# Batch 0's second two pairs turned by VectorE from block loads, with the last ordering, range checks, similarities and slopes at other places

## The chip, the cores and the metric

The kernel runs on one core of a Trainium2 chip. The core has five engines with queues of their own: TensorE (PE in the profile), VectorE (DVE), ScalarE (ACT), GpSimd (POOL) and SyncE (SP), which issues DMAs. [...] The metric is the device time in microseconds. Of the kernel before, three runs took 944.75, 945.04 and 946.84 us; the median is 945.04.

## The reference: what is computed

Routing attention and then a feed-forward block, all in fp32. There are 4 batches, 8 heads, 768 tokens and head dimension 64.

```python
q_n, k_n, c_n = (x / (norm(x) + 1e-6) for x in (q, k, centroids))
q_assign = argmax(q_n . c_n over 16 clusters);  k_assign likewise
scores = where(q_assign[:, None] == k_assign[None, :], q k^T / 8, -1e9)
x = softmax(scores) @ v              # heads side by side: (3072, 512)
h = x @ w_in                         # (3072, 2048)
out = (max(h, 0) + alpha * min(h, 0)) @ w_out    # (3072, 512)
```

A query attends to the keys of its own cluster alone. The weights and alpha are shared by all tokens; the weights come in as 64-bit floating-point numbers.

## The kernel before

**Pairs and steps.** Two heads of one batch make a pair, so there are 16 pairs n, four to a batch; one holds 768 queries and 768 keys of both heads. Pairs 0 to 9 are done whole (all keys against all queries, in two halves of 384 queries), pairs 10 to 15 are first sorted by cluster, so that only near blocks of keys and queries meet. The order of the work is written out by hand: a list of 78 steps (`steps`), three to a half of a pair (or to a sorted pair), 24 for each of the first two batches. A first loop runs steps -4 to 23 (batch 0), a second one steps 24 to 77. In each step pieces are put at slots: `tick()` counts the slots, `later(k, piece)` puts a piece k slots on, `prep_at[(step, slot)]` holds the preparation of pairs to come, `load_at[step]` holds loads, which are issued ahead of everything else in the step. The order in which pieces are emitted is the order on each engine's queue.

**A pair's way through the kernel.** `load` brings q and k of two heads into two tiles of a pool of four (`inp`); `load_v` brings v. The features must lie along the partitions for the scores. For pairs of batch 0 `prep_features` (lines 347 to 359) does this on TensorE, 24 products with an identity matrix in three groups, each copied from PSUM by ScalarE. For pairs of later batches the load writes blocks of 32 features and 32 tokens in such an order (line 127) that `prep_blocks` (364) needs one 32x32 block transpose on VectorE for each of q and k. Batch 0 numbers its tokens as partition times six plus j (the load at line 119 is two contiguous DMAs, one for q and one for k), later batches as j times 128 plus partition. `prep_sims` (381) multiplies features and centroids into a spare PSUM bank of `misc`, and `prep_argmax` finds clusters on VectorE (402 to 410). In batch 0 the members are turned (423), sent to other partitions by small DMAs that ScalarE issues (474), and made into a penalty by ScalarE (429), which TensorE adds to the scores (790). Then come `score` (781), exp on ScalarE (802), `weigh` (936) with sums of the denominators (in batch 0's first halves on TensorE, 929, read by VectorE at 942), and `normalise` (1039), which frees the one PSUM bank of the output products (`vps`) and fills a part of xT. `invert` (904) turns denominators into inverses; `inverse` calls `check_inverses` (340) at the first pair of a new batch, which takes the least and greatest of all inverses for a range check at the end.

**Weights.** They arrive in 32 chunks of 512 KB (`convert`, 247) in five raw tiles. A chunk is split by VectorE (253, 255), scaled by ScalarE (259, 261), joined by VectorE (265, 268) and GpSimd (271). In batch 0 these pieces stand between the attention's own on VectorE's queue; `fetch` issues a chunk's DMA on SP when a raw tile will be free. On SP the order at the start is: loads of pairs 0 and 1, chunks 0 to 2, v of pair 1, load(2), v of pair 2, chunks 3 and 4, load(3), chunks 5 and 6, v of pair 3, chunk 7 and so on.

**Feed-forward.** Once a half batch has its xT, its pieces (`hidden`, 1063, and `final`, 1081) are fed to TensorE between the attention's steps. The last batch's feed-forward works with sums of blocks and fewer products (`last_pieces`, 1241 and 1297). In its `hidden(x)`, two blocks of hidden units, f1 and f2, are made from products p1 to p7 and a deferred p4; `plus` (1176) adds a product from PSUM, `slopes` (1181) applies alpha.

**Sorting.** `ORDERS` gives the step at which a sorted pair's ordering begins: its load (line 127's form), two transposes (565), `order_sims` (573), counts and a scan (587), `order_begins` (599), `order_rows`. This puts 18 stage loads (659, on SP) and 24 scatters (673, on POOL) into a queue, `sorting`, from which the steps take as room allows; `order_load` (694) brings the rows back sorted, before the pair's first step.

Of the kernel before, what the change touches and what calls it, by code (L numbers as in the profile page):

```python
# [19 lines left out]
P = 128  # L20
# [3 lines left out]
def kernel(  # L24
# [11 lines left out]
    nc = tc.nc  # L36

    B, H, S, D = q.shape
    NC = centroids.shape[1]
    DM, DF = moe_w_in.shape  # L40
    NJ = S // P
    NCH = DM // P
# [52 lines left out]
    def later(slots, piece):  # L95
        due.setdefault(now[0] + slots, []).append(piece)
# [7 lines left out]
    pairs = [(b, hp) for b in range(B) for hp in range(NCH)]  # L104
# [3 lines left out]

    Q = 32

    def load(n):

        b, hp = pairs[n]
        for w, src in enumerate((q, k)):
            raw = inp.tile([P, 2, NJ, D], FP32, name="qk")
            if n < NCH:
                nc.sync.dma_start(
                    out=raw.rearrange("p h j d -> p h (j d)"),  # L120
                    in_=src[b, 2 * hp:2 * hp + 2].rearrange("h (p j) d -> p h (j d)",
                                                            j=NJ))
            for h in range(2):
                rows = src[b, 2 * hp + h]
                for x in range(D // Q if n >= NCH else 0):
                    r = h * D + x * Q
                    nc.sync.dma_start(
                        out=raw.rearrange("p h j d -> p (h j d)")[r:r + Q, :].rearrange(
                            "p (t i) -> p t i", i=Q),
                        in_=rows[:, x * Q:(x + 1) * Q].rearrange("(t p) i -> p t i", p=Q))  # L130
            raw_qk[n, w] = raw
# [30 lines left out]
    for g in range(P // Q):  # L162
        r = slice(g * Q, (g + 1) * Q)
        nc.gpsimd.tensor_copy(
            out=fold[r, :].rearrange("p (a i) -> p a i", i=Q),
            in_=ident[r, None, r].broadcast_to((Q, P // Q, Q)))
# [11 lines left out]
    for h in range(2):  # L178
        nc.vector.tensor_reduce(
            out=pick[:, h:h + 1],  # L180
            in_=fold.rearrange("p (a h c) -> p a h c", h=2, c=NC)[:, 0, h, :],
# [142 lines left out]
    lowest = const.tile([P, B], FP32, name="lowest")  # L324
    highest = const.tile([P, B], FP32, name="highest")
    WORDS = [float((127 + e) * 2 ** 23) for e in (-50, 40)]
    kept_of = [0]

    def inverse(n, half):

        if pairs[n][0] > kept_of[0]:
            check_inverses()
        return inverses[:, (2 * n + half) % (2 * NCH), :]

    def check_inverses():
        i = kept_of[0]
        kept_of[0] += 1
        words = inverses.bitcast(I32).rearrange("p n x -> p (n x)")
        for to, op in ((lowest, ALU.min), (highest, ALU.max)):
            nc.vector.tensor_reduce(out=to[:, i:i + 1], in_=words, axis=AX.X, op=op)  # L340
# [20 lines left out]
    def prep_blocks(n, w):  # L361
        if w == 0:
            qkTs[n] = qkp.tile([P, NB * P], FP32, name="qkT")
        nc.vector.transpose(out=qkTs[n][:, w * S:(w + 1) * S],
                            in_=raw_qk[n, w].rearrange("p h j d -> p (h j d)"))
# [11 lines left out]
    def prep_sims(n):  # L377
        hp = pairs[n][1]
        ps = misc()
        for g in range(NG):  # L380
            nc.tensor.matmul(out=ps[g * W:(g + 1) * W, 0:HS],  # L381
                             lhsT=cT[:, hp * W:(hp + 1) * W],
                             rhs=qkTs[n][:, g * HS:(g + 1) * HS],
                             start=True, stop=True)
        later(1, lambda: prep_argmax(n, ps))
# [753 lines left out]
    def last_pieces():  # L1139
        b = B - 1  # L1140
# [34 lines left out]
        def plus(to, of):  # L1175
            nc.vector.tensor_tensor(out=to, in0=to, in1=of, op=ALU.add)

        def slopes(f):
            halves, both = g[f]
            for t in halves if both is None else [both]:  # L1180
                nc.vector.scalar_tensor_tensor(out=t, in0=t, scalar=alpha[:, f:f + 1], in1=t,
                                               op0=ALU.mult, op1=ALU.max)
# [50 lines left out]
        def hidden(x):  # L1233
            f1, f2 = x, NQ + x
            bank = {}

            def product(to, m, rhs, start):
                if start:
                    bank[to] = new_bank(to)[:, 0:HS]
                for cc in range(KH):  # L1240
                    nc.tensor.matmul(out=bank[to], lhsT=w_in_form(m, x, cc),  # L1241
                                     rhs=rhs[:, cc, :], start=start and cc == 0,
                                     stop=cc == KH - 1, skip_group_check=not start)
                return bank[to]

            def x_of(half, kh):
                return xTs[b, half][:, kh * KH:(kh + 1) * KH]

            def g_of(f, half):
                return g[f][0][half]  # L1250

            def p1():
                if not g:
                    places()
                copy(g_of(f1, 0), product("a", "11", x_of(0, 0), True))

            def p5():
                copy(g_of(f2, 1), product("e", "S1", x_sums[0], True))

            def p2():  # L1260
                plus(g_of(f1, 0), product("z", "12", x_of(0, 1), True))
                if late:
                    late.popleft()()

            def p6():
                copy(g_of(f1, 1), product("a", "S2", x_sums[1], False))

            def p3():
                plus(g_of(f1, 1), product("e", "S4", x_of(1, 1), False))
                slopes(f1)  # L1270

            def p7():
                plus(g_of(f2, 1), product("a", "S3", x_of(1, 0), False))
                late.append(p4)
                if x % 2 == 0 and x:
                    g_sums(x - 2)
                    w_out_sums(x - 2)
                    if x // 2 + 1 < NQ // 2:
                        w_in_sums(x // 2 + 1)
                elif x > 1:  # L1280
                    g_sums(x - 2)
                    w_out_sums(x - 2)

            def p4():
                copy(g_of(f2, 0), product("a", "22", x_sums[2], False))
                slopes(f2)
            return [p1, p5, p2, p6, p3, p7]
# [72 lines left out]
    SLOTS, FIRST = 5, 2  # L1360
# [2 lines left out]
    FREE = SLOTS * SB - 3  # L1363


    ORDERS = [26, 29, 35, 38, 41, 50]
    prep_at, load_at = {}, {}
    for (n, half), u in start_of.items():
        def at(step, slot, piece):
            prep_at.setdefault((step, slot), []).append(piece)  # L1370
        if half is None:
            t = ORDERS[n - NO]
            load_at.setdefault(t, []).append(lambda n=n: load(n))
            for i in range(2):
                at(t + 1, FIRST + i, lambda n=n, i=i: order_features(n, i))
            at(t + 2, 2, lambda n=n: order_sims(n))
            load_at.setdefault(u - (3 if n == NO + 1 else 4), []).append(
                lambda n=n: order_load(n))
            at(u - 4, 0, lambda n=n: prep_clusters(n))
            for i in range(2):  # L1380
                at(u - 1, i, lambda n=n, i=i: order_blocks(n, i))
                at(u - 1, FIRST + i, lambda n=n, i=i: order_queries(n, i))
            continue
        if half == 0:
            if n < NCH:
                if n > 1:
                    load_at.setdefault(max(u - 7, 0), []).append(lambda n=n: load(n))
                if n > 0:
                    load_at.setdefault(max(u - 6, 0), []).append(lambda n=n: load_v(n))
            else:  # L1390
                load_at.setdefault(u - 9, []).append(lambda n=n: load(n))
                load_at.setdefault(u - 7, []).append(lambda n=n: load_v(n))
            if n < NCH:
                for g in range(len(groups)):
                    at(u - 4, FIRST + g, lambda n=n, g=g: prep_features(n, g))
            else:
                for w in range(2):
                    at(u - 7, FIRST + w, lambda n=n, w=w: prep_blocks(n, w))
            at(u - (3 if n < NCH else 5 if u - 6 < TOGETHER else 6), FIRST,
               lambda n=n: prep_sims(n))  # L1400
            if n >= NCH:
                at(u - 4, FIRST if u - 4 < TOGETHER else 0, lambda n=n: prep_clusters(n))
        if n < NCH:

            if half == 1 or n == 0:
                at(u - (3 if half else 1), FIRST,
                   lambda n=n, half=half: prep_queries(n, half, 0))
            continue
        for h in range(2):
            at(u - 1, FIRST + h, lambda n=n, half=half, h=h: prep_queries(n, half, h))  # L1410
# [385 lines left out]
```

## Time and profile before

| | |
|---|---|
| profiled execution | 944.23 us, span of its instructions 942.5 us |
| median of three runs | 945.04 us |
| TensorE, VectorE, ScalarE, GpSimd busy | 98%, 70%, 28%, 37% of the span |
| granted TensorE clock | 0.999 |
| line 354, the 192 records of turning by TensorE | 8.6 and 4.2 us busy by tile, 277 and 272 ns each |
| line 364, the 12 transposes of later batches | 11.4 us, 947 ns each |
| line 1063 and 1081, feed-forward products | 257.7 and 254.4 us busy |
| line 340, a check's two reductions | 0.21 to 0.25 us each, first at 224.5, last at 789.8 us |
| queue of SyncE and its engines' share | 201840 packets, 60.35 MB, 29.2% |

A matmul in fp32 appears as two records, so the 24 products of a pair are 48. Records overlap on TensorE: the mean of one is longer than the distance between two. "Idle before" counts from the end of the engine's previous work, and names what ended the wait. An instruction of SP in the timeline is the issue of a DMA; its window is not the transfer. Times in the timeline count from the span's start.

### The profile page before, as it was taken

The numbers are of one execution on the slowest core, as the hardware profiler recorded it, in microseconds if no ns is written. First come the engines' busy times: TensorE is split into PE (matmuls) and PEld (weight loads), VectorE is DVE, ScalarE is ACT, GpSimd is POOL, SyncE is SP. The second block draws the span as 40 slices with busy tenths as digits, with TensorE's granted clock in tenths as the row PEclk, the third lists the DMA queues.
The fourth block names the chain that finished last, engine by engine and source line by source line (L and its number), as shares of the span: only waits on it lengthen the run. The fifth ranks groups of instructions, "written<-read, shape, count | busy, mean of one in ns | idle before, by whom it ended". The sixth has DMA issues, their size and how long they took to land.

```text
span 942.5 us, 11891 instructions
## 1 busy us (share of the span) xinstructions
PE 924.1 (98%) x3995; PEld 496.5 (53%) x3995; DVE 663.5 (70%) x1247; ACT 265.9 (28%) x658; POOL 351.2 (37%) x529
## 2 busy tenths in 40 slices
PE   8999999999999999999999999999999999999997
PEld 5534444445455454454544545545455555556886
DVE  5797788799679589698995955456888535698100
ACT  5764444323123032331322322223133121221000
POOL 2333222200016576467534686364256670000000
PEclk9999999999999999999999999999999999999999
DMA  8333658039001645165920134333441112000000
GB/s 297 125 127 96 146 130 149 18 59 198 1 6 53 159 87 133 47 120 131 155 52 12 43 80 101 63 67 62 93 75 34 32 37 53 1 0 1 23 23 26
DMA packets 209668, 73.38 MB, mean 78 GB/s; under 512 B 194288, under 2 KB 198080, under 8 KB 209600
## 3 DMA queue, kind: packets, MB, share of 16 engines
q1 hardware_dynamic: 201840, 60.35, 29.2%
q0 software_dynamic: 6912, 11.81, 4.1%
q8 instruction: 33, 0.54, 0.2%
q10 hardware_dynamic: 848, 0.39, 0.2%
q14 instruction: 35, 0.29, 0.1%
HBM read 49.89 MB, written 22.28 MB: 77 GB/s over the span
## 4 chain that ended last, share of the span: by engine, by line
PE 87%; DVE 6%; SPq 2%; DMA 2%; issue 1%; POOL 1%; ACT 1%; ACTq 0%; DVEq 0%; POOLq 0%
PE fps L1081 26%; PE fps L1063 25%; PE vps L936 7%; PE sps L781 7%; PE sps L1297 4%; PE sps L1241 4%; PE fps L781 2%; PE vps L1297 2%; PE vps L1241 2%; PE fps L1297 1%; PE fps L1241 1%; PE sps L790 1%; PE vps L969 1%; PE mps L969 1%; PE mps L381 1%
## 5 line engine op out<-in xcount | busy, mean ns | idle before, releaser
L1063 PE MATMUL fps<-xT,w_in_sb 128*128 128x384 f32 x768 | 257.7, 490 | 0.0
L1081 PE MATMUL fps<-w_out_sb,gT 128*128 128x512 f32 x576 | 254.4, 595 | 1.1 <-DVE gT L1055 1.1
L1063 PEld LDWEIGHTS fps<-xT,w_in_sb 128*128 128x128 f32 x768 | 142.8, 190 | 102.6 <-issue 3.8
L1081 PEld LDWEIGHTS fps<-w_out_sb,gT 128*128 128x128 f32 x576 | 107.5, 190 | 133.4 <-issue 123.0
L673 POOL DMA_INDIRECT scratch<-stage,off x144 | 155.4, 1079 | 49.7 <-issue 25.1
L650 POOL COPY paced<-pace 1x1 f32<-1x1 f32 x196 | 55.5, 283 | 202.3 <-ACT pace L649 201.5
L1069 ACT COPY gT<-fps 128x384 f32<-128x384 f32 x96 | 46.0, 479 | 215.6 <-PE fps L1063 215.6
L1055 DVE SCALAR_TENSOR_TENSOR gT<-gT,alpha 128x384 f32<-128x384 f32 x96 | 61.3, 648 | 50.4 <-ACT gT L1069 50.3
L781 PE MATMUL sps<-qkT 64*128 64x384 f32 (+1 forms) x480 | 88.6, 487 | 0.0
L1008 POOL DMA_INDIRECT back<-rows,found x72 | 74.9, 1040 | 18.2 <-issue 16.1
L802 ACT ACTIVATE E<-sps 128x768 f32<-128x768 f32 (+1 forms) x78 | 57.9, 790 | 59.4 <-PE sps L790 38.8
L781 PEld LDWEIGHTS sps<-qkT 64*128 64x128 f32 x480 | 42.7, 186 | 40.5 <-issue 15.0
L822 DVE SCALAR_TENSOR_TENSOR more<-aq,key,more 128x384 f32<-128x384 bf16 (+2 forms) x120 | 63.0, 584 | 1.2 <-ACT more L799 1.1
L936 PE MATMUL vps<-E,vt 128*64 128x384 f32 x316 | 58.6, 495 | 1.4 <-DVE xT L1039 1.4
L904 DVE RECIPROCAL inverses<-mps 64x12 f32<-64x12 f32 (+1 forms) x44 | 10.9, 248 | 58.5 <-PE mps L891 58.1
L822 DVE SCALAR_TENSOR_TENSOR E<-aq,key,E 128x384 f32<-128x384 bf16 (+2 forms) x96 | 50.2, 577 | 1.9 <-ACT E L799 1.8
L271 POOL TENSOR_TENSOR w_in_sb<-w_in_sb,power 128x512 f32<-128x512 f32 x16 | 25.1, 1573 | 67.8 <-DVE w_in_sb L268 67.8
L832 DVE TENSOR_TENSOR acc<-acc,E 128x768 f32<-128x768 f32 x37 | 35.3, 953 | 14.7 <-ACT E L802 13.6
L271 POOL TENSOR_TENSOR w_out_sb<-w_out_sb,power 128x512 f32<-128x512 f32 x16 | 22.9, 1434 | 57.3 <-DVE w_out_sb L268 57.3
L802 ACT ACTIVATE more<-sps 128x768 f32<-128x768 f32 (+1 forms) x42 | 31.1, 775 | 33.1 <-PE sps L781 32.0
L1087 ACT COPY y<-fps 128x512 f32<-128x512 f32 x18 | 10.6, 586 | 99.1 <-PE fps L1081 99.1
L1089 DVE TENSOR_TENSOR y<-y,fps 128x512 f32<-128x512 f32 x24 | 16.4, 683 | 29.1 <-PE fps L1081 29.1
(283 smaller groups left out, 1167.2 us busy)
## 6 DMA issues: line engine op xcount, KB each, us to landing
raw<-in_moe_w_in_dram SPq DMA_DIRECT2D x16, 512.0 KB
raw<-in_moe_w_out_dram SPq DMA_DIRECT2D x16, 512.0 KB
out_dram<-y SPq DMA_DIRECT2D x21, 256.0 KB
qk<-in_q_dram SPq DMA_DIRECT2D x48, 96.0 KB
qk<-in_k_dram SPq DMA_DIRECT2D x48, 96.0 KB
qk<-scratch SPq DMA_DIRECT2D x48, 96.0 KB
w_in_kept<-w_in_sb SPq DMA_DIRECT2D x8, 512.0 KB
vt<-in_v_dram SPq DMA_DIRECT2D x10, 384.0 KB
```

Source lines behind the costliest of these rows:

```text
L650: nc.gpsimd.tensor_copy(out=sorts["paced"], in_=token)
L673: nc.gpsimd.indirect_dma_start(out=scratch[n][1][h * NX + xx], out_offset=bass.IndirectOffsetOnAxis(ap=ranks[n][:, xx, h:h + 1], axis=0), ...
L781: nc.tensor.matmul(out=bank(ps, h, m), lhsT=qkT[r:r + D, S + c * P:S + (c + 1) * P], rhs=qkT[r:r + D, tokens], start=True, stop=not early_ ...
L802: nc.scalar.activation(out=E[:, :, 0:m], in_=ps[:, :, 0:m], func=AF.Exp, scale=SCALE)
L822: nc.vector.scalar_tensor_tensor(out=e, in0=of, scalar=keys[n][:, NJ + c, h:h + 1], in1=e, op0=ALU.is_equal, op1=ALU.mult)
L936: nc.tensor.matmul(out=po[r:r + D, 0:HS], lhsT=vts[n][:, h, c, :], rhs=e[:, h, :], start=(c == 0), stop=(c == NJ - 1))
L1008: nc.gpsimd.indirect_dma_start(out=to[i], out_offset=bass.IndirectOffsetOnAxis(ap=place[:, h, j:j + 1], axis=0), in_=rows[j // HJ][:, j % ...
L1055: nc.vector.scalar_tensor_tensor(out=gs[f], in0=gs[f], scalar=alpha[:, f:f + 1], in1=gs[f], op0=ALU.mult, op1=ALU.max)
L1063: nc.tensor.matmul(out=ps[:, 0:HS], lhsT=w_in_sb[:, c, f * P:(f + 1) * P], rhs=xTs[b, half][:, c, :], start=(c == 0), stop=(c == NCH - 1))
L1081: nc.tensor.matmul(out=ps[:, 0:DM], lhsT=gs[f][:, i * P:(i + 1) * P], rhs=w_out_sb[:, f, :], start=on and f == f0, stop=off and f == f0 + ...
L1241: nc.tensor.matmul(out=bank[to], lhsT=w_in_form(m, x, cc), rhs=rhs[:, cc, :], start=start and cc == 0, stop=cc == KH - 1, skip_group_check ...
L1297: nc.tensor.matmul(out=bank[to], lhsT=g_form(m, x, t), rhs=w_out_form(n, x), start=start and x == 0, stop=x == NQ - 1, skip_group_check=no ...
```

## The change

For pairs 2 and 3 (`NB0 <= n < NCH`), `load` no longer issues one DMA for q and one for k. It issues, for each of the two heads, the two halves of 32 features and the four groups of 32 partitions, a DMA of 32 x 6 pieces of 128 bytes: 16 DMAs for each of q and k. In this layout VectorE's block transpose gives what `prep_features` gave, with the token order of batch 0. So `prep_blocks` takes the place of `prep_features` for these two pairs, at the same step (four ahead of the pair's first) and at two slots in place of three. Pairs 0 and 1 stay as they were.

The ordering of pair 15, the last one, begins at step 54 in place of 50; its load, transposes, similarities and all that follows come four steps later. `check_inverses` for batches 0 to 2 is put three slots after the last inverse of the batch is asked for, in place of ahead of the next batch's first; batch 3's stays at the end. `prep_sims` of pairs 8 and 9 is put one slot later. In the last batch's `hidden`, the slopes of block f1 come after the addition in p7 in place of after the one in p3.

```diff
+    NB0 = 2
+
     def load(n):
         b, hp = pairs[n]
         for w, src in enumerate((q, k)):
             raw = inp.tile([P, 2, NJ, D], FP32, name="qk")
-            if n < NCH:
+            if n < NB0:
                 nc.sync.dma_start(...)
+            for h in range(2 if NB0 <= n < NCH else 0):
+                rows = src[b, 2 * hp + h].rearrange("(g p j) d -> g p j d", p=Q, j=NJ)
+                for x in range(D // Q):
+                    r = h * D + x * Q
+                    to = raw.rearrange("p h j d -> p (h j d)")[r:r + Q, :].rearrange(
+                        "p (j g i) -> p g j i", g=P // Q, i=Q)
+                    for g in range(P // Q):
+                        nc.sync.dma_start(out=to[:, g], in_=rows[g][:, :, x * Q:(x + 1) * Q])
...
-    kept_of = [0]
+    kept_of, inverted = [0], [0] * B
     def inverse(n, half):
-        if pairs[n][0] > kept_of[0]:
-            check_inverses()
+        b = pairs[n][0]
+        inverted[b] += 1
+        if inverted[b] == 2 * NCH and b < B - 1:
+            later(3, check_inverses)
...
             def p3():
                 plus(g_of(f1, 1), product("e", "S4", x_of(1, 1), False))
-                slopes(f1)
             def p7():
                 plus(g_of(f2, 1), product("a", "S3", x_of(1, 0), False))
+                slopes(f1)
...
-    ORDERS = [26, 29, 35, 38, 41, 50]
+    ORDERS = [26, 29, 35, 38, 41, 54]
...
-            if n < NCH:
+            if n < NB0:
                 for g in range(len(groups)):
                     at(u - 4, FIRST + g, lambda n=n, g=g: prep_features(n, g))
             else:
                 for w in range(2):
-                    at(u - 7, FIRST + w, lambda n=n, w=w: prep_blocks(n, w))
+                    at(u - (4 if n < NCH else 7), FIRST + w,
+                       lambda n=n, w=w: prep_blocks(n, w))
             at(u - (3 if n < NCH else 5 if u - 6 < TOGETHER else 6), FIRST,
-               lambda n=n: prep_sims(n))
+               lambda n=n: prep_sims(n)) if u - 6 < 2 * TOGETHER else at(
+                   u - 6, FIRST + 1, lambda n=n: prep_sims(n))
```

## The prediction

> **What bounds the kernel now.** I read the page's busy shares first, then who TensorE waited for, then the order of time on each queue in the first 80 us, where most of the edits land.
>
> ```profile
> PE 924.1 (98%) x3995; PEld 496.5 (53%) x3995; DVE 663.5 (70%) x1247; ACT 265.9 (28%) x658; POOL 351.2 (37%) x529
> ```
>
> TensorE is busy in 924.1 of 942.5 us: whatever TensorE doesn't have to do, and whatever it doesn't wait for, shortens the run, provided that no other queue sets the pace of that stretch. Its waits (engine, line, releaser: us in total, times, longest):
>
> ```profile
> PE fps L354 <- ACT qkT L358: 1.6, 2, 1.5
> PE mps L599 <- DVE simT L587: 1.6, 1, 1.6
> PE vps L936 <- DVE xT L1039: 1.4, 1, 1.4
> ...
> PE mps L381 <- DVE qk L975: 1.2, 1, 1.2
> ...
> PE sps L1241 <- DVE gT L1176: 0.9, 1, 0.9
> PE mps L969 <- DVE inverses L904: 0.9, 1, 0.9
> ```
>
> Each is small; the edits touch L354, L599, L381, L1241 and L969. The timeline of TensorE (start, us, name) shows what turning pair 2 and pair 3 costs now, and the one place where VectorE is late in this part:
>
> ```profile
> 25.76 1.04 PE L354 MATMUL fps<-ident,qk 128*64 128x128 f32 x16
> 26.64 1.04 PE L354 MATMUL mps<-ident,qk 128*64 128x128 f32 x16
> 27.51 1.08 PE L354 MATMUL fps<-ident,qk 128*64 128x128 f32 x16
> ...
> 45.42 1.09 PE L354 MATMUL fps<-ident,qk 128*64 128x128 f32 x16 [1.48 <-ACT qkT L358]
> ...
> 68.02 1.51 PE L936 MATMUL vps<-E,vt 128*64 128x384 f32 x8 [1.42 <-DVE xT L1039]
> ```
>
> VectorE in the same stretch: between the first line below and the last, no idle time is shown, so it sets the pace of these 36 us although TensorE looks full.
>
> ```profile
> 31.74 0.38 DVE L942 STREAM_TRANSPOSE simT<-fps 128x192 f32<-128x192 f32 x1 [3.35 <-PE fps L929]
> ...
> 40.38 0.39 DVE L253 TENSOR_SCALAR power<-raw 128x512 uint32<-128x512 uint32 x1
> ...
> 67.41 0.56 DVE L1039 TENSOR_TENSOR xT<-vps,rd 128x384 f32<-128x384 f32 x1
> ```
>
> And SP's queue, which issues all these loads in program order:
>
> ```profile
> 6.85 0.38 SPq L119 DMA_DIRECT2D qk<-in_q_dram  x1
> ...
> 12.29 0.38 SPq L119 DMA_DIRECT2D qk<-in_q_dram  x1
> 13.64 0.38 SPq L119 DMA_DIRECT2D qk<-in_k_dram  x1
> 23.54 1.55 SPq L247 DMA_DIRECT2D raw<-in_moe_w_out_dram  x2
> ```
>
> The first line is pair 2's q, the next two are pair 3's loads, the last is the fetch of weight chunks 5 and 6, which stand behind them. Chunk 5's split is the VectorE instruction at 40.38 above (the sixth L253).
>
> [...]batch 1's loads in 128 B pieces hold the DMA engines at a share of 0.93 with 148 GB/s (223 to 230 us), against 1.03 with 396 GB/s at 6 to 12 us. [...]issue times hardly follow size (below). [...]
>
> **The change, part by part.**
>
> 1. Pairs 2 and 3 leave TensorE. Removed: 48 records of L354 each, 25.76 to 28.52 (2.76 us) and 42.02 to 46.45 (4.43 us with the 1.48 us wait), 7.2 us together; also three ScalarE copies a pair (0.59 us, off the path). But pair 2's 2.76 us don't come through: the next score also needs the ScalarE-issued copy of pair 1's members, in the chain of waits as "24.55 5.82 DMA aq<-member", so it cannot finish before 30.37, near where it is now. I credit 0.3 us.
>
> 2. Added on VectorE: two 128x768 transposes a pair. L364 of batch 1 is that instruction, median 936 ns, 0.94 each. Pair 2's two (1.9 us) lie in the 3.35 us idle before 31.74; pair 3's two (1.9 us) fall in the stretch without idle, and push the xT at 67.41, so TensorE at 68.02, by 1.9 us. So pair 3's 4.4 us on TensorE gain nothing: TensorE arrives earlier and waits longer. Without any DMA effect this part costs 1.9 - 0.3 = +1.6 us.
>
> 3. Added on SP: each q or k load of these pairs becomes 2 x 2 x 4 = 16 DMAs of 24 KB; 64 instead of 4. This is the unknown. Nearest rows: L119's four median 0.41 (about 0.51 from start to start back to back at 1.25 to 3.29 us); L1020, 96 KB in 128 B pieces,
>
> ```profile
> L1020 SPq DMA_DIRECT2D qk<-back x24: 303/518/580, 523.6 to 782.1; - x24
> L474 ACTq DMA_DIRECT2D aq<-member x14: 514/600/614, 23.9 to 137.2; - x14
> ```
>
> and even a 24 KB move of 32 partitions (L474) takes 0.60. With 0.04 between issues that is 0.51 to 0.65 each whatever the size; I take 0.56. If small blocks were cheaper than every row shown, a lone issue's 0.30 would be the lower end. Behind these issues on SP stand load_v(2), chunks 3 and 4, load(3), then chunks 5 and 6. From 6.85: backlog of the 1.5 MB of weights just issued 2 us (0 to 3; batch 1's first four issues behind two weight chunks took 3.18 instead of 2.04), 64 x 0.56 = 35.8, the three others 1.3: chunk 5 is issued at 46.0 instead of 23.54. Landing: 2.4 us as the stage loads in the chain, plus about 0.6 for eight times their size: 49.0. VectorE wants it at about 40.1 and stands there for 9 us. Queued behind on VectorE: joins of chunks 3 and 4, pair 3's transposes, the denominators of pair 1 (49.29), its xT, all up to pair 2's xT. TensorE waits for them at weigh (first_den and the single vps bank). From chunk 5's split to the end of that xT is 67.97 - 40.38 = 27.6, with pair 3's transposes 29.4: xT at 78.4 where TensorE now resumes at 68.02. **+10.4 us** (this contains the +1.6). Ends: 0.51 an issue, no backlog, landing 2.4: +4.7; 0.65, backlog 3, landing 3.5: +17.7. Chunk 3 and pair 2's k come late too (about 30 instead of 26), but before chunk 5, so they are not added. After 68 TensorE is the bound again, with two waits of 0.9 and 0.3 up to 260, so nothing is won back.
>
> 4. Range checks. Two reductions of 0.25 us each leave the place ahead of the reciprocals. At 473.6 TensorE waits 0.93 for these (L969): -0.4. The one near 224.5 lies in idle time: 0. Without cover later: +0.5.
>
> 5. prep_sims of pairs 8 and 9 one slot later: the 1.16 wait of L381 at 479.61 was for a bank that normalise had not left. -1.1; at worst 0, if what is next then waits.
>
> 6. Last ordering from step 50 to 54: moves load(15)'s eight issues (468.5 to 473.4 on SP) into a time when SP issues nothing (475.9 to 523.6), two 0.97 us transposes, the argmax pieces, the scan, order_begins with the 1.58 us wait at 517.74, and order_rows; then 6 x 3 stage loads and 24 scatters on POOL. The scatters keep their place: 51 of the 144 start after 500 us and the last pair's 24 are the end of that queue (from about 592), while order_rows moves only from 521 to about 545. -1.6 to 0, I take -1.0: the wait may return at its new place, although VectorE has idle time at 545 to 562 (8.96 of 17 us busy).
>
> 7. Slopes of the first block after the next addition. At 861.68 TensorE waits 0.95 for L1176; the slopes ahead of it in p3 (0.6) go behind it: -0.7 (0 to -0.9).
>
> Sum: +10.4 - 0.4 - 1.1 - 1.0 - 0.7 = +7.2. The profiled execution took 944.23 (span 942.5 and 1.7 around it), 0.8 below the median of 945.04, which is the spread of the three runs; on the median that is **952 us**.
>
> **The rivals.** A difference under 0.2% (943.2 to 946.9) I call no change.
> A, above: SP late by the issues, chunk 5 late. Own range 947 to 957.5. Chance 0.64.
> B, not slower: an issue of a small block takes 0.42 us or less from start to start. Then chunk 5 is issued by 37.1 (6.85 + 2 + 1.3 + 64 x 0.42) and lands by 40.1, and only part 2's +1.6 stays against -3.2 of parts 4 to 7: 943.4, or 942.4 with their full -4.2. For it: the lone 0.30. Against: no row back to back is under 0.5. Chance 0.11, half of it under 943.2.
> C: between, 0.45 an issue: some +4 from chunk 5 and -4: 945. Against it the same rows. Chance 0.07.
> D: heavier. The 128 B pieces also hold up ScalarE's member copies (5.82 us to landing already), or SP must wait for landings before it reissues: 0.7 an issue, some +19 less 4: 960. Against: at 148 GB/s a 24 KB block is 0.17 us of the engines, so they keep up. Chance 0.11.
> E, faster: B's cheap issues, and VectorE has slack that I don't see between 31 and 68 us, so that TensorE keeps its 7.2: -7.2 - 3.2, 934.6. Against: the wait at 68.02 is already VectorE's. Chance 0.07.
>
> **How the numbers follow.** Predicted is A's 952. From 942.5 (all but the end of B, and E: 0.09 below) to 959 (most of D: 0.1 above). Faster by over 0.2%: E and half of B, 0.13. Within: half of B, most of C, 0.12. Slower: 0.75.
>
> **What would show it.** Right: 64 issues of q and k blocks on SP at 0.5 to 0.65, ending near 45; the chunk 5 split on VectorE waiting for a DMA into raw near 40 to 49; TensorE's wait for L942 or L1039 growing to several us between 46 and 80; waits of L381 and L599 near 480 and 517 gone. Wrong: issues near 0.4, VectorE never waiting for raw. B then holds; if TensorE also keeps its 7 us (E), my reading of VectorE as the pace of 31 to 68 us was wrong.

## The result and the profile after

| | before | after |
|---|---|---|
| median | 944.98 us (944.75 to 946.84, 4 runs) | 966.93 us (966.73 to 967.15, 4 runs) |
| profiled execution, span | 944.23, 942.5 us | 967.04, 965.3 us |
| granted TensorE clock | 0.999 | 0.985 |

The ratio is 1.0228, with a 95% interval of 1.021 to 1.0246: slower by 22 us. 952 was predicted, with a range up to 959. In the new file a line number is 8 higher than before from line 127 up to about line 335 and 10 higher from there on (line 354 is now 364, 790 is 800, 936 is 946); the plain load, line 119, is 118. The runs further below have small shifts of their own. The page of the changed kernel, busy shares:

```profile
PE 927.9 (96%) x3899; PEld 494.0 (51%) x3899; DVE 665.8 (69%) x1251; ACT 262.6 (27%) x652; POOL 352.3 (37%) x529
```

TensorE has 96 records fewer, as meant, and yet 3.8 us more of busy time (924.1 before): what is left runs at a granted clock of 0.985 for 0.999. What TensorE waited for (us in total, times, longest):

```profile
PE sps L791 <- ACT E L812: 14.7, 1, 14.7
PE sps L800 <- DMA aq<-member: 5.6, 3, 5.2
PE mps L1009 <- DVE simT L412: 3.4, 1, 3.4
PE vps L946 <- DVE xT L1049: 1.7, 1, 1.7
...
PE sps L1251 <- DVE gT L1186: 0.6, 1, 0.6
```

The waits of L354, L599, L381 and L969 from the prediction are gone or small. One of 14.7, one of 5.2 and one of 3.4 us have come. The first begins in SP's queue (start and length of the issues, us):

```profile
7.11 13.67 SPq L130 DMA_DIRECT2D qk<-in_q_dram  x16
20.89 11.22 SPq L130 DMA_DIRECT2D qk<-in_k_dram  x16
...
33.83 11.36 SPq L130 DMA_DIRECT2D qk<-in_q_dram  x16
45.29 10.62 SPq L130 DMA_DIRECT2D qk<-in_k_dram  x16
56.02 1.01 SPq L255 DMA_DIRECT2D raw<-in_moe_w_out_dram  x2
```

The four loads of pairs 2 and 3 take 13.67 + 11.22 + 11.36 + 10.62 = 46.87 us of SP, 0.73 an issue, and chunk 5 leaves at 56.0 where it left at 23.5. The timelines of VectorE, ScalarE and TensorE show its way on:

```profile
60.04 0.43 DVE L261 TENSOR_SCALAR power<-raw 128x512 uint32<-128x512 uint32 x1 [13.23 <-DMA raw<-in_moe_w_out_dram]
...
60.50 0.72 ACT L267 ACTIVATE power<-power,low_exp 128x512 uint32<-128x512 uint32 x1 [16.34 <-DVE power L261]
...
62.49 2.93 PE L791 MATMUL sps<-qkT 64*128 64x384 f32 x8 [14.69 <-ACT E L812]
...
88.68 1.51 PE L946 MATMUL vps<-E,vt 128*64 128x384 f32 x8 [1.70 <-DVE xT L1049]
```

VectorE stands 13.2 us before chunk 5's split. ScalarE's scaling of that chunk waits for the split, and the exps of the scores (L812) stand behind it in ScalarE's queue; so TensorE, which has no free bank for scores, stands 14.7 us. Pair 2's values (L936 before, 68.02) start at 88.68: **+20.7 us**. The windows of this stretch (start:end, length, then busy us of TensorE, weight load, VectorE, ScalarE and GpSimd, then granted clock, DMA share, GB/s) show a second cost:

```profile
56.00:62.00 6.00, 0.00 (x0) 0.00 (x0) 1.96 (x5) 1.50 (x3) 0.00 (x0) 0.50 0.86 281
62.00:68.00 6.00, 5.51 (x34) 2.28 (x36) 6.00 (x7) 3.95 (x6) 4.57 (x3) 0.63 0.78 242
```

During the idle time the clock falls to 0.50, at about 53 us, 5 us after TensorE's last product. It is 0.50 from 62 to 66 us and 1.00 from 67 on (0.63 on average over these 6 us): TensorE is back at work at 62.49, and the clock is up some 4 us later. The eight scores at 62.49 take 2.93 us; with the clock up, eight take 1.56. In pair2_blocks, a run described below, slow products follow a wait of only 2.67 us: sixteen of turning take 1.50 us (51.55) for 1.04, and the eight scores behind them 2.79.

The other loss lies at the moved ordering, on TensorE:

```profile
544.90 0.85 PE L583 MATMUL mps<-qk,cT 128*32 128x384 f32 x8
549.19 0.90 PE L1009 MATMUL mps<-ident,qk 128*128 128x128 f32 x3 [3.44 <-DVE simT L412]
549.89 5.08 PE L1073 MATMUL fps<-xT,w_in_sb 128*128 128x384 f32 x8
```

The turn of the rows (L1009) wants the small bank that the similarities of pair 15 (L583) have just filled; VectorE empties it (L412) only after masks, sums and slopes that stand ahead. The wait is 3.44 us, and the feed-forward's eight products behind it take 5.08 us instead of 2.85.

How much follows such a wait differs from run to run. Eight traces show this same wait of 3.4 us at this place and the products behind it; these eight take 2.75, 2.75, 3.86, 3.96, 4.03, 4.29, 4.44 and, in the changed kernel, 5.08 us. In pair3_blocks, a run described below, no slow stretch follows:

```profile
538.68 0.55 PE L1009 MATMUL mps<-ident,qk 128*128 128x128 f32 x3 [3.44 <-DVE simT L412]
539.07 2.75 PE L1073 MATMUL fps<-xT,w_in_sb 128*128 128x384 f32 x8
```

So about 2.2 us of the changed kernel's time at this place are not the wait itself, and another execution may not pay them.

How far like instructions of the two profiles lie apart says where the 22.8 us of span come from:

| TensorE instruction (line before) | before | after | apart |
|---|---|---|---|
| values of pair 2 (936) | 68.02 | 88.68 | +20.7 |
| feed-forward (1081) | 194.59 | 215.25 | +20.7 |
| values behind batch 1's check (969) | 474.90 | 494.88 | +20.0 |
| scores behind part 5's wait and the ordering's old similarities (781) | 508.18 | 526.14 | +18.0 |
| turn of the rows behind the old wait of L599 (999) | 520.84 | 536.74 | +15.9 |
| scores behind the ordering's new place (781) | 531.91 | 554.90 | +23.0 |
| the last batch's blocks (1241) | 861.68 | 884.82 | +23.1 |

So parts 1 to 3 cost 20.7 us instead of 10.4, and parts 4 to 7 together cost 2.1 instead of gaining 3.2. These 2.1 are of one execution, with the slow stretch of 2.2 us in it.

### The profile page after: what moved, and what is told of

Read it like the earlier page. It is cut to its first block, busy times and chain, and to the rows that moved or that the text cites. A ratio compares the mean times of both kernels' runs of the same rounds, so it can differ in the third digit from the quotient of the medians.

```text
span 965.3 us, 11765 instructions
## 1 busy us (share of the span) xinstructions
PE 927.9 (96%) x3899; PEld 494.0 (51%) x3899; DVE 665.8 (69%) x1251; ACT 262.6 (27%) x652; POOL 352.3 (37%) x529
## 4 chain that ended last, share of the span: by engine, by line
PE 86%; DVE 7%; DMA 3%; SPq 2%; issue 1%; ACT 0%; DVEq 0%; ACTq 0%
PE fps L1091 26%; PE fps L1073 23%; PE vps L946 8%; PE sps L791 7%; PE sps L1251 4%; PE sps L1307 4%; PE fps L791 3%; SPq L130 2%; PE vps L1307 2%; PE vps L1251 2%; PE fps L1307 1%; PE fps L1251 1%; DMA vt<-in_v_dram 1%; PE mps L979 1%; PE sps L800 1%
## 5 line engine op out<-in xcount | busy, mean ns | idle before, releaser
L791 PE MATMUL sps<-qkT 64*128 64x384 f32 (+1 forms) x480 | 89.9, 494 | 14.7 <-ACT E L812 14.7
L812 ACT ACTIVATE E<-sps 128x768 f32<-128x768 f32 (+1 forms) x78 | 57.9, 790 | 59.9 <-PE sps L800 40.6
L842 DVE TENSOR_TENSOR acc<-acc,E 128x768 f32<-128x768 f32 x37 | 35.2, 952 | 14.7 <-ACT E L812 13.6
L279 POOL TENSOR_TENSOR w_out_sb<-w_out_sb,power 128x512 f32<-128x512 f32 x16 | 22.8, 1423 | 58.5 <-DVE w_out_sb L276 58.5
L812 ACT ACTIVATE more<-sps 128x768 f32<-128x768 f32 (+1 forms) x42 | 31.1, 776 | 32.6 <-PE sps L791 31.5
L946 PEld LDWEIGHTS vps<-E,vt 128*64 128x64 f32 x316 | 20.4, 138 | 28.3 <-issue 25.4
```

The costliest lines, as they stand in the source:

```text
L791: nc.tensor.matmul(out=bank(ps, h, m), lhsT=qkT[r:r + D, S + c * P:S + (c + 1) * P], rhs=qkT[r:r + D, tokens], start=True, stop=not early_ ...
L812: nc.scalar.activation(out=E[:, :, 0:m], in_=ps[:, :, 0:m], func=AF.Exp, scale=SCALE)
L946: nc.tensor.matmul(out=po[r:r + D, 0:HS], lhsT=vts[n][:, h, c, :], rhs=e[:, h, :], start=(c == 0), stop=(c == NJ - 1))
```

## The experiments

Each ratio is to runs of the kernel before, made beside it (medians 944.67, 946.05, 945.63 and 944.75 in the four groups of runs).

| run | what it is | median, us | ratio, 95% interval |
|---|---|---|---|
| plain_loads | changed kernel, pairs 2 and 3 loaded as before | 948.07 | 1.0061 (1.0033 to 1.009) |
| tensor_turn | changed kernel, pairs 2 and 3 loaded and turned as before | 948.24 | 1.0027 (1.0017 to 1.0037) |
| order50 | changed kernel, ordering back at 50 | 964.51 | 1.0203 (1.0186 to 1.022) |
| spare_issues | kernel before, with 60 more issues | 968.94 | 1.0264 (1.0241 to 1.0287) |
| pair3_blocks | only pair 3 in blocks | 957.55 | 1.0124 (1.01 to 1.0147) |
| pair2_blocks | only pair 2 in blocks | 957.08 | 1.0104 (1.0077 to 1.0131) |
| k_four | k of pairs 2 and 3 in four DMAs | 955.45 | 1.01 (1.0076 to 1.0123) |
| pair3_pool | pair3_blocks, two copies issued by GpSimd | 957.24 | 1.012 (1.0091 to 1.0149) |
| after_pool | changed kernel, the same edit | 967.67 | 1.0237 (1.0208 to 1.0266) |
| chunks_first | changed kernel, chunks 5 and 6 ahead of load(3) | 960.75 | 1.0175 (1.0147 to 1.0203) |
| chunks_pool53 | that, with both edits and ordering at 53 | 958.16 | 1.0138 (1.0111 to 1.0164) |
| small_edits | parts 4, 5 and 7 alone | 944.51 | 0.9985 (0.9971 to 1.0) |
| order53 | those, and ordering at 53 | 943.69 | 0.9982 (0.9974 to 0.9989) |
| order52 | those, and ordering at 52 | 946.37 | 1.0004 (0.9994 to 1.0013) |

### The issues alone, and the turning alone

spare_issues leaves the changed kernel's edits out and adds, behind each of the four loads, 15 block DMAs into a place that nothing reads at that time:

```diff
+            for y in range(15 if 2 <= n < NCH else 0):
+                ...
+                nc.sync.dma_start(out=spare..., in_=rows[g][:, :, x * Q:(x + 1) * Q])
```

> The kernel before, turned by TensorE, with 15 block DMAs added behind each of the four loads of pairs 2 and 3, into a part of the weights' memory that is overwritten later: the issues of the change without its turning. Theory S: 945 + 18 to 21 = 963 to 966 us, chunk 5 issued near 54 us. Theory V: 945 to 947 us.

plain_loads does the reverse, VectorE's turning without the block loads. The features of pairs 2 and 3 are then in a wrong order, and the work is the same.

```diff
-            if n < NB0:
+            if n < NCH:
                 nc.sync.dma_start(...)
-            for h in range(2 if NB0 <= n < NCH else 0):
-                ...
```

> The changed kernel, but pairs 2 and 3 are loaded by one DMA each for q and k as before, and still turned by VectorE; so their features are not the right ones (the blocks lie in another order), all else is done in full. Theory S (64 issues on SP make weight chunk 5 late): chunk 5 is issued near 24 us again, VectorE never waits for it; 944 to 949 us, of which +2 are the other edits as the trace of the change shows them. Theory V (VectorE's two extra transposes a pair in a stretch without idle time): stays above 955 us.

tensor_turn sets `NB0 = 4`, so that neither is there, and all later edits are.

> The changed kernel with pairs 2 and 3 loaded and turned by TensorE as before: only the last ordering, range checks, similarities and slopes remain changed. By the offsets between the two traces (+20.7 us up to 215 us, +22.8 at the end) these four together cost +2: 947 us. If my working before the run were right on them: 942 us. If they, not the loads, carry the loss: above 960 us.

The issue of chunk 5 and 6 and the waits in spare_issues:

```profile
57.84 1.01 SPq L256 DMA_DIRECT2D raw<-in_moe_w_out_dram  x2
```

```profile
PE fps L363 <- ACT qkT L367: 20.6, 2, 15.6
...
DVE power L262 <- DMA raw<-in_moe_w_out_dram: 14.1, 1, 14.1
```

The added DMAs alone, with nothing moved off TensorE, give 968.94, the whole loss: chunk 5 leaves at 57.8, VectorE waits 14.1 us for it, and TensorE 5.0 and 15.6 us where it turns pair 2 and pair 3, in place of the changed kernel's 5.2 and 14.7. They bring 60 transfers of 24 KB with them as well as 60 issues; k_four below tells the two apart. Without the block loads, in plain_loads, TensorE starts pair 2's values where it did before:

```profile
67.59 1.51 PE L937 MATMUL vps<-E,vt 128*64 128x384 f32 x8 [1.71 <-DVE xT L1040]
```

In tensor_turn they start at 67.68. Turning two pairs on VectorE thus neither gains nor costs at that place, and the two medians are 0.2 us apart. Over the whole kernel that is less sure: three of the seven executions of plain_loads took 952.6 to 954.6, longer than any of the twenty of tensor_turn, and the kept trace is of one that took 947.52. TensorE's freed time came back as small waits (for qkT 1.6, for aq 1.6, for E 0.6 us).

### One pair, and fewer issues

If the loss is chunk 5's lateness alone, it should have a threshold: with 32 issues instead of 64, chunk 5 should come almost in time, and nearly nothing should be lost.

```diff
-    NB0 = 2
+    IN_BLOCKS = {3}
...
-            if n < NB0:
+            if n < NCH and n not in IN_BLOCKS:
```

> The changed kernel with only pair 3 loaded in blocks and turned by VectorE; pair 2 as before. 32 issues instead of 64, from 12.3 us on. If the loss begins only where chunk 5 comes later than VectorE wants it (about 40 us): chunk 5 is issued near 35, lands near 39, no wait for it, and the time is that of the kernel with all four pairs turned by TensorE (948), within 1.5 us. If the loss is in proportion to the issues: 957 to 958 us.

pair2_blocks is the same with `{2}`:

> The changed kernel with only pair 2 loaded in blocks and turned by VectorE; pair 3 as before. Chunk 5 is issued near 35 as above, but pair 2's k (wanted at 26 us) and chunk 3 land at about 32 and 37 us, and the member copy of pair 1 waits for one of the block loads: TensorE is some 6 us late at 38 us and stays so: 952 to 955 us. If chunk 5 alone matters: 948 us.

k_four loads k (and v) of both pairs in the token order of later batches, so that k takes four DMAs and q sixteen: 40 issues with the same bytes.

> The changed kernel with k of pairs 2 and 3 loaded by 4 DMAs of 96 KB, its keys and v in the token order of the later batches; q stays in 16. The bytes and the 128 byte pieces are the same, the issues are 40 instead of 64. If issues set the time: SP is done near 39 us instead of 56, chunk 5 lands near 43, 2 to 4 us late: 949 to 952 us. If the 128 byte pieces set it: 967 us.

k_four lies between, as issues and not bytes would have it, but above its expectation. SP's queue there, ending in chunks 5 and 6:

```profile
24.65 13.56 SPq L130 DMA_DIRECT2D qk<-in_q_dram  x16
38.31 2.25 SPq L135 DMA_DIRECT2D qk<-in_k_dram  x4
40.66 0.94 SPq L255 DMA_DIRECT2D raw<-in_moe_w_out_dram  x2
```

Four DMAs of 96 KB take 2.25 us, 0.56 each; sixteen of 24 KB take 13.56, 0.85 each with the gaps between them (0.60 in the median for the issue itself). Pair 2's values start at 73.46. And pair3_blocks refutes chunk 5 as the only link: chunk 5 leaves at 38.15, VectorE waits for no chunk, and the time is still 957.55, where the rival of a loss in proportion to the issues had put it. In pair2_blocks, too, VectorE doesn't wait for chunk 5 (issued at 34.5), but 5.5 us for pair 2's k and 3.0 for the chunk behind that; the values start at 75.77, and 957.08 is above both expectations. The timelines of ScalarE, TensorE and VectorE in pair3_blocks:

```profile
29.37 1.23 ACTq L484 DMA_DIRECT2D aq<-member  x2
30.65 1.29 ACT L439 ACTIVATE outside<-member,pick 64x384 bf16<-64x384 bf16 x2 [5.35 <-DMA qk<-in_k_dram]
...
32.60 1.98 PE L364 MATMUL fps<-ident,qk 128*64 128x128 f32 x16 [4.94 <-ACT qkT L368]
...
39.19 0.38 DVE L952 STREAM_TRANSPOSE simT<-fps 128x192 f32<-128x192 f32 x1 [10.86 <-PE fps L939]
```

ScalarE's issue of pair 1's member copies (23.91 before) comes at 29.37, and ScalarE is said to wait 5.35 us for a DMA into qk, which those copies don't touch; everything behind them in ScalarE's queue waits too. SP issues pair 3's blocks of q from 13.07 and those of k from 27.80, so the copies come out while k's first blocks are on their way. In the changed kernel it is the same, at 30.34 and with a wait of 6.48 us for k's blocks of pair 2 (issued from 20.89). What ties a copy that ScalarE issues to a block that SP issues, the traces don't show. That the delay hangs on who issues the copies can be tried.

### Is it the copies that ScalarE issues?

```diff
-                        nc.scalar.dma_start(out=to, in_=members[n][0][r, :])
+                        (nc.gpsimd if n == 1 else nc.scalar).dma_start(
+                            out=to, in_=members[n][0][r, :])
```

GpSimd takes pair 1's two copies over from ScalarE. The edit was made to pair3_blocks and to the changed kernel.

> Only pair 3 in blocks and turned by VectorE, and pair 1's two copies of members into aq are issued by GpSimd instead of ScalarE[...]. [...]the copies go out near 24 us instead of 29.4, ScalarE's wait of 5.35 us, TensorE's of 4.94 us and VectorE's of 10.86 us between 29 and 39 us are gone, the values of pair 2 start near 68 instead of 76.45, and the time is 947 to 950. Rival, that the sixteen-row pieces themselves or SP's late third load hold the pipeline: unchanged, 956 to 959, with the values of pair 2 at 75 or later.

> The changed kernel with that edit alone. Chunk 5 of the weights, still issued behind 64 block loads at about 56 us, decides: VectorE's wait for it stays near 13 us, the values of pair 2 stay at 87 to 89, and the time is 964 to 968. [...]

TensorE and VectorE in pair3_pool:

```profile
28.08 1.08 PE L364 MATMUL fps<-ident,qk 128*64 128x128 f32 x16
...
42.75 0.43 DVE L261 TENSOR_SCALAR power<-raw 128x512 uint32<-128x512 uint32 x1 [2.12 <-DMA raw<-in_moe_w_out_dram]
...
45.20 1.62 PE L791 MATMUL sps<-qkT 64*128 64x384 f32 x8 [2.82 <-ACT E L812]
...
71.40 2.83 PE L946 MATMUL vps<-E,vt 128*64 128x384 f32 x8 [1.71 <-DVE xT L1049]
```

The three waits between 29 and 39 us are gone, although GpSimd issues the copies only at 27.78, behind work of its own, and L364 runs at 28.08 instead of 32.60: the copies, issued late by ScalarE, held the pipeline there. What they had hidden shows now: chunk 5, issued at 38.9, is 2.1 us late. Pair 2's values start at 71.40, 5.1 earlier than in pair3_blocks, not at 68 as expected. Of the 5.1 us 4.9 are still there at 479 us, 2.8 at 536 and 1.2 at 873: a wait of 2.3 us for `more` at 485, which pair3_blocks doesn't have, took the first part. The second part goes at the turn of the rows: both runs wait 3.44 us there, and the slow stretch follows in pair3_pool alone (3.96 us for the eight products, 2.75 in pair3_blocks); the lead falls from 2.8 to 1.3. The four executions range from 952.5 to 959.5 us, and their median is not lower than that of pair3_blocks and lies where the rival had it. So this second coupling is shown at its place and not in the total. In the full change, after_pool, the copies no longer matter (967.67): chunk 5, later still, decides.

### Chunk 5 first

The last question was whether chunk 5's place behind the 64 issues carries the loss. Pair 3's load was put one step later, which changes nothing but SP's order: chunks 5 and 6 now leave ahead of it.

```diff
-                    load_at.setdefault(max(u - 7, 0), []).append(lambda n=n: load(n))
+                    load_at.setdefault(max(u - (7 if n < 3 else 6), 0), []).append(
+                        lambda n=n: load(n))
```

> The changed kernel with pair 3's block loads placed one step later, so that the loads of chunks 5 and 6 stand ahead of them in SP's queue; the order of every other engine is the same. Theory, chunk 5 carries it: it is issued near 34 us instead of 56, VectorE's wait of 13.2 us for it is gone, and since the last piece of pair 3's k now lands near 60 us and VectorE wants it near 55, a wait of up to 5 us comes in its place; the values of pair 2 at 74 to 80, the time 952 to 960. Rival, the 64 issues cost the same in any order: 963 or more.

> The same, with pair 1's two copies into aq issued by GpSimd and the last ordering at 53. Without the 3.4 us wait for simT and its slow clock: 5 to 6 us under the run with the chunks first alone, 947 to 954. It stays above the 943.7 of the later edits alone, because pair 2's k still comes 6 us later than VectorE wants it.

SP, VectorE and TensorE in chunks_first:

```profile
33.12 1.50 SPq L255 DMA_DIRECT2D raw<-in_moe_w_out_dram  x3
34.72 13.51 SPq L130 DMA_DIRECT2D qk<-in_q_dram  x16
48.32 11.74 SPq L130 DMA_DIRECT2D qk<-in_k_dram  x16
```

```profile
62.08 0.98 DVE L374 STREAM_TRANSPOSE qkT<-qk 128x768 f32<-128x768 f32 x1 [6.71 <-DMA qk<-in_k_dram]
...
63.12 1.49 PE L391 MATMUL mps<-qkT,cT 128*32 128x384 f32 x4 [7.93 <-DVE qkT L374]
...
84.52 1.51 PE L946 MATMUL vps<-E,vt 128*64 128x384 f32 x8 [1.71 <-DVE xT L1049]
```

The wait for chunk 5 is gone, and a wait of 6.7 us for pair 3's k has taken its place, because the queue still ends at 60 us (and then one of 2.1 us for chunk 7, which is issued behind it at 60.80). The time, 960.75, lies between the theory (952 to 960) and the rival (963 or more), and the values at 84.52 later than the theory's 74 to 80: chunk 5 is the last link but not the cause. The cause is that SP takes 47 us for what were four issues of 0.38 us; whatever stands last comes late. chunks_pool53 at 958.16, above its expected 947 to 954, says the same with pair 1's copies issued by GpSimd and without the wait at the turn of the rows.

### The later edits

small_edits keeps parts 4, 5 and 7 (`NB0 = 4`, ordering at 50); order50 is the changed kernel with only the ordering back; order53 and order52 are small_edits with other steps for it.

```diff
-    ORDERS = [26, 29, 35, 38, 41, 54]
+    ORDERS = [26, 29, 35, 38, 41, 53]
```

> The changed kernel with the last ordering back at step 50. If the 3.4 us wait of TensorE for the similarities of the last pair, and the slower clock after it, come from the move: 962 to 964 us, and that wait is gone. If the wait has another cause: 967 us.

> The changed kernel with pairs 2 and 3 loaded and turned as before and the last ordering at step 50: only the range checks, the similarities of pairs 8 and 9 and the slopes stay moved. From the traces: -0.7 for the checks, -0.3 for the slopes, -1.2 for the similarities if no new wait follows, +0.4 if TensorE then waits for a bank that ScalarE still reads: 943 to 944.5 us.

> The later edits alone with the last ordering at 53 instead of 54: all pairs are loaded plain and turned by TensorE. If the wait of 3.4 us for simT belongs to place 54 only, because the turn of the rows there needs the one small bank right behind the ordering of the last pair, it is gone, the wait of 1.6 us on the other simT is gone too or under 1 us, and the time is 942 to 945. If the ordering meets the same reader one step earlier, the wait stays at 2 us or more and the time is 946 to 949.

> The same with the last ordering at 52. Between 50 (944.5 measured, one wait of 1.6 us) and 54 (948.2, one of 3.4): 942.5 to 945.5. No wait over 2 us on simT at the turn of the rows; if there is one, 946 to 949.

At 54 (tensor_turn, 1.0027) the ordering costs 0.4% against 50 (small_edits, 0.9985), 4 us; order50 gets 2.4 us of it back in the changed kernel. small_edits itself can't be told from no change: its interval ends at 1.0. TensorE at that place in tensor_turn, and then in order53:

```profile
517.96 7.91 PE L1073 MATMUL fps<-xT,w_in_sb 128*128 128x384 f32 x24
525.80 0.85 PE L583 MATMUL mps<-qk,cT 128*32 128x384 f32 x8
530.09 0.74 PE L1009 MATMUL mps<-ident,qk 128*128 128x128 f32 x3 [3.44 <-DVE simT L412]
```

```profile
519.71 1.06 PE L583 MATMUL mps<-qk,cT 128*32 128x384 f32 x8 [0.62 <-ACT rows L1012]
520.70 8.01 PE L1073 MATMUL fps<-xT,w_in_sb 128*128 128x384 f32 x24
528.54 0.49 PE L1009 MATMUL mps<-ident,qk 128*128 128x128 f32 x3
```

One step earlier, the 8 us of feed-forward products stand between the two users of the bank instead of ahead of both, and VectorE has emptied it in time. order53 has neither this wait nor the one at L609 and is the only run with an interval below 1: 943.69, 0.18% under before, which is at the edge of what can be told from no change. At 52 the L609 wait (1.5 us) is back; 946.37 is no gain and above its expectation. Its profiled execution took 943.71, so the scatter of these runs (943.7 to 948.6) is as large as what is asked of them.

## Why the prediction was wrong in its size

**What held.** Direction and mechanism: SP's issues delay chunk 5, VectorE stands before its split, and TensorE waits until pair 2's xT. The chain from split to xT took 28.6 us (predicted 29.4). Nothing of it was won back after 68 us.

**Part 3, the term that failed: the price of an issue, and SP's waits between issues.** It put 64 issues at 0.56 with 2 us of backlog, 37.8 us; they took 46.9. Chunk 5 was predicted at 46.0 and left at 56.0; its landing was taken as 3.0 us and took 4.0. So +10.4 becomes 10.4 + 10.0 + 1.0 - 0.8 = +20.6, against 20.7 seen.

The 46.9 us have two parts. The issues themselves take 0.60 in the median, with 0.04 to the next: 41.3 us in all (one issue of 1.56 us among them), 5.5 more than predicted. The row of the same shape, L474 (24 KB on 32 partitions, 0.60), had been shown, and I averaged it down with rows of larger DMAs; the upper end of 0.65 would have been right. The other 5.5 us are ten longer gaps, 3.8 us of them in the first load, where the prediction had 2 us of backlog, 3 at most. SP's list of waits (us in total, times, longest) says what SP waits for ahead of the block loads:

```profile
SPq L130 <- DMA raw<-in_moe_w_in_dram: 3.2, 4, 1.0
...
SPq L130 <- DMA vt<-in_v_dram: 0.7, 2, 0.5
...
SPq L130 <- DMA qk<-in_k_dram: 0.5, 1, 0.5
...
SPq L130 <- DMA qk<-in_q_dram: 0.4, 1, 0.4
...
SPq L130 <- DMA raw<-in_moe_w_out_dram: 0.2, 1, 0.2
```

These are landings, 5.0 us together, most of them of weight chunks, which the blocks don't touch. They are nine waits in 64 issues; a block lands 2.1 us after its issue in the median. Why a block waits for another DMA's landing is not shown.

Rival D had named this link ("SP must wait for landings before it reissues"), and ScalarE's late member copies too (30.34 us here, 23.91 before). Its 0.7 an issue was nearly the right figure (0.73, gaps included), and its +19 nearly the right sum. It does not hold in full: the waits for landings are 5 of the 46.9 us, and D's other reason, that the small pieces hold up the transfers, is not seen: the DMA engines are at a share of 0.24 (20 to 32 us). The larger part is the price of the issue itself. Why a block of 24 KB takes SP longer than one of 96 KB stays open.

**What part 3 left out.** ScalarE's copies, which come out late beside SP's blocks: in pair3_blocks 5 us at pair 2's values, in the full change hidden behind chunk 5. And the clock: the idle time of 14.7 us is followed by some 4 us at a clock of 0.50, which at 62.49 costs 1.4 us for one group of scores alone. At that place VectorE's chain ends later still and covers it; at the ordering nothing does.

**Parts 1 and 2.** +1.6 was given; plain_loads against tensor_turn measures -0.1 at pair 2's values. Pair 3's two transposes do lie in VectorE's stretch and cost it 0.9 us, not 1.9. But the stretch begins 1.0 us earlier (at 30.36 for 31.36), because TensorE no longer turns pair 2, for which 0.3 had been credited; so its end did not move.

**Part 4** was right: -0.7 for -0.4. **Part 5** holds in the changed kernel: the 1.16 us wait is gone, and nothing stands in its place. In small_edits and tensor_turn a wait for `more` of 1.17 and 1.62 us does, which the prediction had as its bound ("at worst 0, if what is next then waits"). **Part 7**: the wait fell from 0.95 to 0.65, -0.3 for -0.7. Together small_edits gains 0.15%, 1.4 us, where 2.2 were predicted, with an interval that reaches no change.

**Part 6** had the wrong sign. It asked whether VectorE had idle time at the new place and whether the old wait would return there, and not which other instruction takes the small bank directly behind the ordering's. At the old place 2.9 us went: the similarities (0.85), the wait of 1.58 and the products at L599 themselves. At the new one 7.1 came (+15.9 to +23.0): the similarities, a wait of 3.44 at L1009, and eight products 2.2 us longer at the slow clock behind it. That is +4.2, for a predicted -1.0; of it the 2.2 of the slow clock are what this execution happened to get, so that between +2 and +4 stands against the prediction.

## What to carry to other kernels

Count a load's DMAs and price them as issues by the row of the same shape, add the waits for the landings that they queue behind (5.0 us of SP here), and ask what stands last in that queue: here blocks that left the DMA engines at a share of 0.24 (20 to 32 us) held three engines through one queue, and another order only chose what was late. Ask also which single copies of another engine fall into such a burst: ScalarE's copies came at 29.37 us in pair3_blocks for 23.91 before. When a piece moves, list who else takes its bank next, and give a TensorE wait a range and not its length alone: here the slow stretch behind one of 3.4 us cost between nothing and 2.3 us.

## What the runs showed of the hardware

- An issue of 24 KB on 32 partitions takes 0.60 us of SP in the median, 0.64 from start to start back to back. That is longer than one of 96 KB in pieces of the same 128 bytes (2.25 us for four, 0.56 from start to start).
- With the gaps between them, waits for earlier landings among these, the small issues came at 0.64 us each (k of pair 3 in pair3_blocks) to 0.92 (q of pair 3 in pair3_pool).
- ScalarE's issue of pair 1's two copies came at 23.91 us before, at 29.37 in pair3_blocks and at 30.34 in the changed kernel. With GpSimd issuing them in pair3_pool, ScalarE's wait of 5.35 us was gone.
- After waits of 3.4 us TensorE's next eight feed-forward products took from 2.75 us (no slow stretch) to 5.08. In the changed kernel the clock was 0.54 from 550 to 555 us. In pair2_blocks a wait of only 2.67 us was followed by eight scores in 2.79 us, which take 1.56 elsewhere. A short wait can cost more than its length.
